# Where ScalarE's decode operations stand in an attention slot: attention and two feed-forward layers on one core

## The chip, the cores and the metric

The kernel runs on 1 core of one Trainium2 chip. The metric is the device time of one execution in microseconds; the value for a kernel is the median of its runs. Times of single instructions come from one profiled execution.

## What is computed

Block-causal attention (4 batches, 8 heads, 576 positions, head size 64) is followed by two feed-forward layers over 2304 tokens of width 512, each with a hidden width of 2048. All of it is float32.

```python
scores = scale * np.matmul(q, k.transpose(0, 1, 3, 2))
mask = block_i >= block_j                       # blocks of 64
scores = np.where(mask, scores, -1000000000.0)
attn = np.exp(scores - np.max(scores, axis=-1, keepdims=True))
attn = attn / (np.sum(attn, axis=-1, keepdims=True) + 1e-09)
x = np.matmul(attn, v)                          # then heads side by side: (2304, 512)
h = x @ w_in                                    # layer 1
x = (np.maximum(h, 0.0) + alpha * np.minimum(h, 0.0)) @ w_out
h = x @ w_in2                                   # layer 2
out = np.where(h > 0.0, h, np.exp(np.minimum(h, 0.0)) - 1.0) @ w_out2
```

## The kernel before

**Weights and their decode.** The host hands each weight matrix over as pairs of 32-bit words, two words to an element, the low one and the high one of a 64-bit number. The kernel makes of them two tiles in the matmul's own number format, a high part and a low part. It does so in 64 pieces of 128 x 512 elements (16 hidden chunks, two layers, `w_in` and `w_out`), each by one call of `load_w`. A piece is a load (SyncE's queue, tile `wraw`, three buffers) and then eight operations on three engines, in this order: ScalarE's `Abs` of the high words into the word tile `wword` (line 133) and its conversion of the low words in place (line 134), together `first`; VectorE's two bit operations (`bits`, lines 138 and 139) and the sign (`sign`, line 143); GpSimd's addition (`rounded`, line 148); ScalarE's cast to the high part `w` (line 158); VectorE's subtraction for the low part (`last`, through line 89). The `wraw` buffer is free again after GpSimd's addition, the `wword` buffer after the subtraction. There are two `wword` buffers.

**When the operations are written.** `later(ticks, emit)` puts an operation off by so many ticks. A tick ends with each attention slot, and with each step of the feed-forward work. So in the attention part `first` of a piece stands at the end of one slot, `bits` and `sign` at the end of the next, `rounded` at the end of the one after, the cast at the end of the fourth and the subtraction at the end of the fifth.

**Attention.** 64 slots, each one tile of scores of one pair of heads. `slot(k)` writes, in this order: the scores on TensorE (into one of two PSUM tiles, `twin`); the products of probabilities and values of an earlier slot (`second`, line 423); the transposes of an earlier slot's probabilities (`transposes`); the parts of late keys; `normalise` of an earlier slot (VectorE's sum and reciprocal, GpSimd's scaling of `p`); the maxima on VectorE (line 298); the held gates of layer 1; the output of the products, which is ScalarE's cast to `x` (line 429) and VectorE's low part (line 89); the copy `move` of the transposed probabilities `pt`, half on ScalarE and half on VectorE (lines 93 and 95); the exponentials on ScalarE (line 325); and what is planned for the slot's end, the due decode operations last. In this part the order of every engine is that in which the code is written. The first 16 slots are the short ones (two 128-row tiles of a pair); in the 48 that follow, tiles of 384, 512 and 576 columns take turns. From slot 14 on, `l1_beside` puts matmuls of layer 1 between the slots. Sixteen pieces of weights are decoded in the attention part, at the slots in `w_slots`.

**Feed-forward.** From about 258 us on only TensorE's order is the one written; on the other engines a scheduler, working with a model of the times when the kernel is built, puts the operations in order under the limits of the buffers. Layer 1 runs in passes A, B and D over units of 512 (one of 256) tokens, layer 2 in pass C. Each step multiplies one chunk (lines 551, 605), applies the gate (lines 528 to 535) or the exponential (609 to 614), and three steps later multiplies by `w_out` into one of five PSUM accumulators (lines 655, 630). At the end of a unit of pass A the four accumulators are copied out to `z` and `zl` (`to_z`, lines 93 on ScalarE and 95 on VectorE); at the end of a unit of B or D they are added to the earlier sum (line 662 on VectorE). The next unit's second accumulator is one that such a copy has to empty first.

`later` and the point in `load_w` that the change concerns:

```python
lead = arrival[0]
later(lead, first)
...
later(lead + 3, lambda: act.copy(hi, word[0]))
later(lead + 4, last)
```

Of the kernel before, what the change touches and what calls it, by code (L numbers as in the profile page):

```python
# [9 lines left out]
F32 = mybir.dt.float32  # L10
# [4 lines left out]
ALU = mybir.AluOpType  # L15
# [4 lines left out]
P = 128  # L20
B, H, S, D = 4, 8, 576, 64
NT, DM, DFF = 2304, 512, 2048
# [14 lines left out]
def f32(ap):  # L37
    return ap.bitcast(F32)
# [3 lines left out]
def attention_moe_kernel(ctx: ExitStack, tc: tile.TileContext, qT, kT, v_a, v_b, w1, w2, alpha, out):  # L42
    nc = tc.nc
    pe, act, dve, pool_e = nc.tensor, nc.scalar, nc.vector, nc.gpsimd
# [4 lines left out]
    wraw_p = ctx.enter_context(pool("wraw", 2))  # L49
# [18 lines left out]
    def ring(name, *banks):  # L68
        rings[name] = list(banks)
# [18 lines left out]
    def low_part(eng, out, x, high):  # L88
        return {"v": dve, "p": pool_e}[eng].tensor_tensor(out=out, in0=x, in1=f32(high), op=ALU.subtract)  # L89

    def copy(eng, out, x, scale=None):
        if eng == "a":
            return act.copy(out, x) if scale is None else act.mul(out, x, scale)  # L93
        if eng == "v":
            return dve.tensor_copy(out, x) if scale is None else dve.tensor_scalar(out, x, scale, None, ALU.mult)
        return pool_e.tensor_scalar(out, x, 1.0 if scale is None else scale, 1.0, ALU.mult, ALU.mult)  # L96
# [6 lines left out]
    def later(ticks, emit):  # L103
        due.setdefault(tick[0] + ticks, []).append(emit)
# [13 lines left out]
    def load_w(layer, f, r):  # L118
        if r == 0:
            wt[layer, f] = w_pools[min(f // 4, 2)].tile([P, 2, 2 * DM], F32R, tag="w", name="w")  # L120
        t = wt[layer, f]
        raw = wraw_p.tile([P, 2 * DM], U32, tag="wraw", name="wraw", bufs=3)
        nc.sync.dma_start(out=raw, in_=(w1, w2)[layer][f, :, r * DM:(r + 1) * DM].bitcast(U32))
        pairs = raw.rearrange("p (n t) -> p n t", t=2)
        low, high = pairs[:, :, 0], pairs[:, :, 1]
        units = low.bitcast(I32)
        hi, lo = (t[:, k, r * DM:(r + 1) * DM] for k in range(2))
        word = []

        def first():  # L130
            w = wraw_p.tile([P, DM], F32, tag="wword", name="wword")
            word.append(w)
            act.activation(out=w, in_=high.bitcast(F32), func=AF.Abs)  # L133
            act.activation(out=units, in_=low, func=AF.Copy, scale=2.0 ** -29)

        def bits():
            w, wi = word[0], word[0].bitcast(U32)
            dve.tensor_scalar(w, w, F64_MIN, F64_MAX, ALU.max, ALU.min)  # L138
            dve.tensor_scalar(wi, wi, 3, 0x3FFFFFF8, ALU.logical_shift_left, ALU.bitwise_and)  # L139

        def sign():
            wi = word[0].bitcast(U32)
            dve.scalar_tensor_tensor(  # L143
                out=wi, in0=high, scalar=0xC0000000, in1=wi, op0=ALU.bitwise_and, op1=ALU.bitwise_or)

        def rounded():
            w = word[0].bitcast(I32)
            pool_e.tensor_tensor(out=w, in0=w, in1=units, op=ALU.add)  # L148

        def last():  # L150
            low_part("v", lo, word[0], hi)
            ready.add((layer, f, r))
        lead = arrival[0]
        later(lead, first)
        later(lead + 1, bits)
        later(lead + 1, sign)
        later(lead + 2, rounded)
        later(lead + 3, lambda: act.copy(hi, word[0]))  # L158
        later(lead + 4, last)

    arrival = [2]

    def w_in(layer, f, part, kc):
        assert (layer, f, 0) in ready
        return wt[layer, f][:, part, kc * P:(kc + 1) * P]
# [17 lines left out]
    ap2 = att.enter_context(pool("att2", 2))  # L183
# [18 lines left out]
        return d // 2, slice(4 * (d % 2), 4 * (d % 2) + 4)  # L202

    def raw_tiles():
        return [ap2.tile([P, S], F32, tag=f"{x}raw", name=f"{x}raw", bufs=4) for x in "qk"]

    def load_early(d):
        b, hs = duo(d)
# [15 lines left out]
    def load_late(n):  # L224
        b, p = PAIRS[n]
        st[n]["raw"] = q, k = raw_tiles()
        hs = slice(2 * p, 2 * p + 2)
        nc.sync.dma_start(out=k, in_=kT[b, hs].rearrange("e p s -> (e p) s"))
        nc.sync.dma_start(out=q[:, 256:], in_=qT[b, hs].rearrange("e p s -> (e p) s")[:, 256:])

    def load_late_v(n):
        b, p = PAIRS[n]
# [5 lines left out]
    def high_parts(n):  # L238
        s = st[n]
        q, k = s["raw"]  # L240
        for which, x, scale in (("q", q[:, 256:], 0.125), ("k", k, None)):
            s[which] = [ap2.tile([P, x.shape[1]], F32R, tag=f"{which}{t}", name=f"{which}{t}") for t in "hl"]
            copy("p", s[which][0], x, scale)
        low_part("p", s["k"][1], k, s["k"][0])

    def low_parts(n):
        s = st[n]
        hi, lo = s["q"]
        dve.scalar_tensor_tensor(out=lo, in0=s["raw"][0][:, 256:], scalar=0.125, in1=f32(hi), op0=ALU.mult, op1=ALU.subtract)

    def diagonal(n):
        for low in range(2):
# [41 lines left out]
    def maxima(n, i):  # L294
        s = st[n]
        s["stat", i] = stat = stats[AT[n, i] % len(stats)]
        sb = s["sb", i]
        peak = lambda out, x, axis=AX.X: dve.tensor_reduce(out=out, in_=x, axis=axis, op=ALU.max, negate=True)  # L298
        if i == EARLY:
            dve.memset(sb[:64].rearrange("p x (t c) -> p x t c", t=2)[:, :, :, 64:P], NEG)  # L300
            for t, lo, hi in EARLY_TILES:
                peak(stat[:, 2 * t:2 * t + 2], sb[:, :, lo:hi])
        elif i < 4:
            ext = P * (i + 1)
            dve.memset(sb[:64, :, ext - 64:ext], NEG)
            peak(stat[:, 0:2], sb[:, :, :ext])
        else:
            peak(stat[:, 0:1], sb[:, :, :S // 2], AX.XY)
# [133 lines left out]
    for n in range(NP):  # L442
        k = AT[n, EARLY]
# [3 lines left out]
        for i in (2, 3, 4):  # L447
            k = AT[n, i]
# [12 lines left out]
    for n in range(NP):  # L461
        k = NP + 3 * n
# [10 lines left out]
    held = []  # L473

    def slot(k):
        here = SEQ[k] if k < NS else None
        if here:
            scores(*here)
        shared.clear()
        outs = [p() for p in products_at.get(k, ())]  # L480
        move = transposes(*transposes_at[k]) if k in transposes_at else None
        for emit in SPLITS.get(k, ()):
            emit()
        for emit in NORM.get(k, ()):
            emit()
        if here:
            maxima(*here)
        after = [h() for h in held]
        held.clear()
        for o in outs:  # L490
            o()
        if move:
            move()
        if here:
            exponentials(*here)
        for a in after:
            a()
        for emit in other_at.get(k, ()):
            emit()
        end_tick()  # L500
# [168 lines left out]
    with tc.manual_schedule(engines={ET.PE, ET.Activation, ET.DVE, ET.Pool, ET.SP}):  # L669
        ring("s", 0, 1)  # L670
        ring("t", 4, 5, 6, 7)

        halves = [(0, f, r) for r in range(2) for f in range(FA)]
        load_early(0)
        load_early(1)
        for half in range(2):
            scale_early(0, slice(256 * half, 256 * half + 256), "v")
        load_early_v(0)
        load_alpha()
        for emit in other_at[-1]:  # L680
            emit()
        load_early_v(1)
        end_tick()
        LEAD = 14
        stretches = [(LEAD, 22, 22, 30), (30, 39, 39, X_DONE[2]), (X_DONE[2], 59, 59, LAST)]
        w_slots = {1, 3, 6, 8, 10, 12, 14, 16}
        w_slots |= {27 + 5 * i for i in range(8)}
        halves += [(0, FA + f, r) for r in range(2) for f in range(4)]

        def slots(lo, hi):  # L690
            for k in range(lo, hi):
                if k in w_slots:
                    arrival[0] = 4 if k > 21 else 2
                    load_w(*halves.pop(0))
                slot(k)

        slots(0, LEAD)

        k = LEAD
        for u, (a, b, c, d) in enumerate(stretches):  # L700
            assert a >= X_DONE[u]
            parts = l1_beside(u)
            for first, end, n in ((a, b, 2 * FA), (c, d, 2 * KC)):
                slots(k, first)
                k = first
                for j in range(n):
                    next(parts)
                    to = first + (2 * (j + 1) * (end - first) + n) // (2 * n)
                    slots(k, to)
                    k = to  # L710
        arrival[0] = 2
        assert not held and not halves


    with tc.manual_schedule(engines={ET.PE}):
# [20 lines left out]
        for i in range(16):  # L736
            f, r = divmod(i, 2)
# [3 lines left out]
        for i in range(len(steps) + lag):  # L741
# [3 lines left out]
            if i < len(steps):  # L745
                k, u, f = steps[i]
                if f == fs[k][1]:
                    n = units.index((k, u)) + 1
# [4 lines left out]
            if i >= lag:  # L753
                k, u, f = steps[i - lag]
# [37 lines left out]
```

## Time and profile before

| | |
|---|---|
| median of 3 runs | 1006.86 us (1006.80 to 1007.06) |
| the profiled execution's own time | 1007.81 us |
| its span | 1006.0 us |
| TensorE matmul busy | 961.3 us (96%), 5008 matmuls |
| VectorE busy | 541.1 us (54%) |
| ScalarE busy | 441.9 us (44%) |
| GpSimd busy | 343.9 us (34%) |
| granted TensorE clock, mean | 0.989 |

The span is the time between the first and the last instruction of the profile; the execution's own time has 1.8 us around it. Busy shares are means over parts with different limits, so the argument goes by stretches of the span: from the start to about 70 us, on to the end of attention at about 258 us, and the feed-forward part behind it. In a list of instructions the columns are the start, the time, the engine, the line and operation with the tiles written and read, and in brackets the idle time of the engine just before with the engine and line that ended it.

### The profile page before, as it was taken

How to read it: one execution, taken by the hardware profiler on the slowest of the kernel's cores; microseconds unless marked ns; L12 is line 12 of the kernel's file. 1: busy time of each engine (PE TensorE's matmuls, PEld its weight loads, DVE VectorE, ACT ScalarE, POOL GpSimd, SP SyncE). 2: the span in 40 equal slices, each digit the busy share in tenths (PEclk: the TensorE clock that was granted, in tenths of full speed). 3: DMA queues.
4: the chain of work that ended last, by engine and by line, in shares of the span. 5: the costliest groups of instructions: out<-in, count | busy, mean ns of one | idle time of the engine just before them, and what ended most of it. 6: DMA issues, size and time to landing. Idle time of an engine off the chain costs nothing.

```text
span 1006.0 us, 13778 instructions
## 1 busy us (share of the span) xinstructions
PE 961.3 (96%) x5008; PEld 774.1 (77%) x5008; DVE 541.1 (54%) x1012; ACT 441.9 (44%) x985; POOL 343.9 (34%) x401
## 2 busy tenths in 40 slices
PE   5789999999997999999999999999999999999997
PEld 3456777666787788888889887888888888888896
DVE  5878676776498871311862489634333333333343
ACT  6876576776465653222553365422222222222222
POOL 4788576694255553322553363200000000000000
PEclk9999999999998999999999999999999999999999
DMA  6553533625546552401535555002002100200010
GB/s 216 178 183 140 154 102 114 224 72 157 183 140 237 199 183 84 141 0 42 186 119 177 163 201 174 29 1 111 15 1 84 42 1 1 84 1 0 1 43 21
DMA packets 55525, 105.76 MB, mean 105 GB/s; under 512 B 11041, under 2 KB 29473, under 8 KB 54305
## 3 DMA queue, kind: packets, MB, share of 16 engines
q1 hardware_dynamic: 55168, 104.62, 31.4%
q8 instruction: 39, 0.64, 0.3%
q10 hardware_dynamic: 288, 0.26, 0.1%
q14 instruction: 30, 0.24, 0.1%
HBM read 76.55 MB, written 28.31 MB: 104 GB/s over the span
## 4 chain that ended last, share of the span: by engine, by line
PE 73%; DVE 11%; ACT 6%; DMA 4%; POOL 3%; issue 2%; SPq 0%; POOLq 0%; ACTq 0%; DVEq 0%
PE bank L630 20%; PE bank L605 19%; PE bank L655 11%; PE bank L551 11%; PE bank L423 3%; PE bank L582 3%; DMA wraw<-w 2%; DVE w L89 2%; PE bank L570 2%; DVE wword L143 2%; PE pair L276 2%; DVE wword L139 2%; PE bank L363 2%; DVE wword L138 1%; ACT wword L133 1%
## 5 line engine op out<-in xcount | busy, mean ns | idle before, releaser
L605 PE MATMUL bank<-x,w 128*128 128x512 f32 (+1 forms) x960 | 210.4, 368 | 0.0
L605 PEld LDWEIGHTS bank<-x,w 128*128 128x128 f32 x960 | 169.7, 189 | 31.4
L551 PE MATMUL bank<-x,w 128*128 128x512 f32 (+1 forms) x816 | 177.2, 367 | 1.3 <-DVE xtail L89 1.3
L551 PEld LDWEIGHTS bank<-x,w 128*128 128x128 f32 x816 | 143.0, 191 | 26.2 <-ACT xtail L429 1.4
L610 DVE TENSOR_SCALAR e<-e 128x512 f32<-128x512 f32 (+1 forms) x80 | 33.1, 413 | 172.1 <-ACT e L609 172.1
L609 ACT ACTIVATE e<-bank 128x512 f32<-128x512 f32 (+1 forms) x80 | 44.4, 555 | 184.8 <-PE bank L605 184.8
L148 POOL TENSOR_TENSOR wword<-wword,wraw 128x512 int32<-128x512 int32 x64 | 93.7, 1465 | 77.3 <-issue 23.5
L531 DVE SCALAR_TENSOR_TENSOR g<-neg,beta,bank 128x512 f32<-128x512 f32 (+1 forms) x80 | 55.1, 689 | 117.8 <-ACT neg L528 117.7
L630 PE MATMUL bank<-w,gsl 128*128 128x512 f32 x432 | 106.4, 393 | 2.2 <-DVE z L662 2.2
L630 PE MATMUL bank<-w,gs 128*128 128x512 f32 x432 | 104.6, 389 | 0.0
L655 PE MATMUL bank<-gsl,w 128*128 128x512 f32 (+1 forms) x408 | 91.0, 371 | 9.1 <-ACT z L93 6.5
L96 POOL TENSOR_SCALAR p<-p,stat 128x128 f32<-128x128 f32 (+4 forms) x144 | 81.3, 580 | 48.5 <-DVE stat L334 32.7
L630 PEld LDWEIGHTS bank<-w,gsl 128*128 128x128 f32 x432 | 81.2, 190 | 19.5 <-DVE z L662 2.6
L630 PEld LDWEIGHTS bank<-w,gs 128*128 128x128 f32 x432 | 80.6, 188 | 16.4
L89 POOL TENSOR_TENSOR gs<-g,gs 128x512 fp32r<-128x512 f32 (+1 forms) x46 | 59.0, 1283 | 90.0 <-ACT gs L535 89.9
L655 PEld LDWEIGHTS bank<-gsl,w 128*128 128x128 f32 x408 | 71.7, 192 | 23.0 <-ACT z L93 7.1
L325 ACT ACTIVATE p<-pair,stat 128x128 f32<-128x128 f32 (+4 forms) x144 | 78.3, 557 | 24.0 <-DVE stat L298 21.7
L655 PE MATMUL bank<-gs,w 128*128 128x512 f32 (+1 forms) x408 | 87.8, 364 | 0.0
L655 PEld LDWEIGHTS bank<-gs,w 128*128 128x128 f32 x408 | 70.6, 189 | 12.2
L528 ACT ACTIVATE neg<-bank 128x512 f32<-128x512 f32 (+1 forms) x80 | 44.1, 552 | 79.5 <-PE bank L551 78.3
L89 DVE TENSOR_TENSOR w<-wword,w 128x512 fp32r<-128x512 f32 x64 | 57.1, 896 | 16.5 <-ACT w L158 15.9
L298 DVE TENSOR_REDUCE stat<-pair 128x2 f32<-128x256 f32 (+3 forms) x80 | 63.1, 806 | 4.2 <-PE pair L281 2.2
(80 smaller groups left out, 1256.7 us busy)
## 6 DMA issues: line engine op xcount, KB each, us to landing
wraw<-w SPq DMA_DIRECT2D x64, 512.0 KB, 4.0
xd<-x SPq DMA_DIRECT2D x4, 2048.0 KB, 8.5
x<-xd SPq DMA_DIRECT2D x16, 512.0 KB, 7.6
x<-yd SPq DMA_DIRECT2D x4, 2048.0 KB, 7.9
vraw<-v_a SPq DMA_DIRECT2D x24, 256.0 KB, 3.3
kraw<-kT SPq DMA_DIRECT2D x16, 288.0 KB, 3.8
yd<-gs SPq DMA_DIRECT2D x8, 512.0 KB, 3.7
yd<-gsl SPq DMA_DIRECT2D x8, 512.0 KB, 5.4
```

Source lines behind the costliest of these rows:

```text
L89: return {"v": dve, "p": pool_e}[eng].tensor_tensor(out=out, in0=x, in1=f32(high), op=ALU.subtract)
L96: return pool_e.tensor_scalar(out, x, 1.0 if scale is None else scale, 1.0, ALU.mult, ALU.mult)
L148: pool_e.tensor_tensor(out=w, in0=w, in1=units, op=ALU.add)
L298: peak = lambda out, x, axis=AX.X: dve.tensor_reduce(out=out, in_=x, axis=axis, op=ALU.max, negate=True)
L325: act.activation(out=out, in_=x, func=AF.Exp, bias=stat[:, k:k + 1], accum_out=stat[:, SUMS + 2 * k:SUMS + 2 * k + 1])
L528: act.activation(out=neg, in_=h, func=AF.Relu, scale=-1.0)
L531: dve.scalar_tensor_tensor(out=g, in0=neg, scalar=beta[:, f:f + 1], in1=h, op0=ALU.mult, op1=ALU.add)
L551: pe.matmul(h, w_in(0, f, wp_, kc), x[:, xp_, kc, :n], start=kc == 0 and t == 0, stop=kc == KC - 1 and t == 2)
L605: pe.matmul(h, w_in(1, f, wp_, kc), x[:, xp_, kc, :], start=kc == 0 and t == 0, stop=kc == KC - 1 and t == 2)
L609: act.activation(out=e, in_=h, func=AF.Exp)
L630: pe.matmul(acc, gs[:, gp_, tg * P:(tg + 1) * P], w_out(1, f, wp_, 0, DM), start=f == 0 and t == 0, stop=f == NF - 1 and t == 2)
L655: pe.matmul(acc, w_out(0, f, wp_, m * P, P), gs[:, gp_, :n], start=first and t == 0, stop=last and t == 2)
```

## The change

`first` and the cast of a piece no longer stand at a slot's end. When they come due, they are put on a list `amid`; the next slot writes what is on the list between `move` and the exponentials. The bit operations, the sign and the addition come due as many ticks after `first` as before, the subtraction one tick after the cast. Outside the attention slots (`in_slots` false) the list is passed by and the operations are written at once. Beside that the word tile has three buffers in place of two, and the raw query tile is 512 columns wide in place of 576, which makes the room: late queries go to columns 0 to 319 in place of 256 to 575.

```diff
         def first():
-            w = wraw_p.tile([P, DM], F32, tag="wword", name="wword")
+            w = wraw_p.tile([P, DM], F32, tag="wword", name="wword", bufs=3)
...
-        lead = arrival[0]
-        later(lead, first)
-        later(lead + 1, bits)
-        later(lead + 1, sign)
-        later(lead + 2, rounded)
-        later(lead + 3, lambda: act.copy(hi, word[0]))
-        later(lead + 4, last)
+
+        def begin():
+            first()
+            later(1, bits)
+            later(1, sign)
+            later(2, rounded)
+            later(3, lambda: between(cast))
+
+        def cast():
+            act.copy(hi, word[0])
+            later(1, last)
+        later(arrival[0], lambda: between(begin))
 
     arrival = [2]
+    amid, in_slots = [], [True]
+
+    def between(emit):
+        if in_slots[0]:
+            amid.append(emit)
+        else:
+            emit()
...
-        return [ap2.tile([P, S], F32, tag=f"{x}raw", name=f"{x}raw", bufs=4) for x in "qk"]
+        return [ap2.tile([P, n], F32, tag=f"{x}raw", name=f"{x}raw", bufs=4) for x, n in (("q", 512), ("k", S))]
...
-        nc.sync.dma_start(out=q[:, 256:], in_=qT[b, hs].rearrange("e p s -> (e p) s")[:, 256:])
+        nc.sync.dma_start(out=q[:, :320], in_=qT[b, hs].rearrange("e p s -> (e p) s")[:, 256:])
...
         if move:
             move()
+        todo = amid[:]
+        amid.clear()
+        for emit in todo:
+            emit()
         if here:
             exponentials(*here)
...
-        assert not held and not halves
+        assert not held and not halves and not amid
+        in_slots[0] = False
```

Three places show what it does to ScalarE's order. TensorE's order is the same in both kernels.

The first is slot 8, where the cast of one piece and `first` of another fall together. `x` is the cast of the products' output, `pt` the copy of transposed probabilities, `p` the exponentials. ScalarE before:

```order
L325 ACTIVATE p_406,stat_124<-pair_102,stat_124 128x256 x2
L158 CAST w<-wword 128x512
L133 ACTIVATE wword<-wraw 128x512
L134 ACTIVATE wraw<-wraw 128x512
L429 CAST x_318<-bank_105 128x256
L93 COPY pt<-bank_106 128x2x256
L325 ACTIVATE p_446,stat_125<-pair_101,stat_125 128x128 x2
```

The same place of ScalarE now (the lines have other numbers: 158 is 162, 325 is 337, 429 is 441):

```order
L337 ACTIVATE p_406,stat_124<-pair_102,stat_124 128x256 x2
L441 CAST x_315<-bank_105 128x256
L93 COPY pt<-bank_106 128x2x256
L162 CAST w<-wword 128x512
L133 ACTIVATE wword<-wraw 128x512
L134 ACTIVATE wraw<-wraw 128x512
L337 ACTIVATE p_446,stat_125<-pair_101,stat_125 128x128 x2
```

The three decode operations moved behind `x` and `pt`; the same operations stand ahead of the exponentials as before.

The second is slot 17, on ScalarE as well (`neg` and `gs` belong to layer 1). Before:

```order
L528 ACTIVATE neg<-bank_103 128x512
L158 CAST w<-wword 128x512
L133 ACTIVATE wword<-wraw 128x512
L134 ACTIVATE wraw<-wraw 128x512
L429 CAST x_655<-bank_105 128x256
L93 COPY pt<-bank_104 128x2x256
L325 ACTIVATE p_879,stat_128<-pair_102,stat_128 128x512 x2
```

And now:

```order
L544 ACTIVATE neg<-bank_103 128x512
L441 CAST x_654<-bank_105 128x256
L93 COPY pt<-bank_104 128x2x256
L162 CAST w<-wword 128x512
L133 ACTIVATE wword<-wraw 128x512
L134 ACTIVATE wraw<-wraw 128x512
L337 ACTIVATE p_879,stat_128<-pair_102,stat_128 128x512 x2
```

Here too the cast of the decode (158, now 162) no longer stands ahead of `x` and `pt`.

The third is in pass A, where the scheduler sets the order: ScalarE around the copies `z` of the 512-token unit's accumulators. Before:

```order
L133 ACTIVATE wword<-wraw 128x512
L134 ACTIVATE wraw<-wraw 128x512 x2
L528 ACTIVATE neg<-bank_2977 128x256
L93 COPY z<-bank_2971 128x512
L158 CAST w<-wword 128x512
L535 CAST gsl<-g 128x256
L93 COPY z<-bank_2973 128x512
```

And now:

```order
L133 ACTIVATE wword<-wraw 128x512
L134 ACTIVATE wraw<-wraw 128x512
L544 ACTIVATE neg<-bank_2977 128x256
L162 CAST w<-wword 128x512
L93 COPY z<-bank_2971 128x512
L93 COPY z<-bank_2973 128x512
L551 CAST gsl<-g 128x256
```

A cast of the decode moved ahead of the first `z`, and the second `z` ahead of the gate's cast. Counted from the start of pass A to VectorE's first copy `zl` of this unit, VectorE's order holds 26 bit operations, 12 signs and 13 subtractions now, 22, 11 and 11 before. From there to the first `zl` of the 256-token unit it holds 16, 9 and 9 now, 16, 7 and 8 before; and from the two subtractions that open pass D's second unit to the first addition of line 662 at its end, 23, 11 and 13 now, 21, 10 and 11 before.

## Rows read from the trace of the kernel before

**Rows 1.** Stretches; columns: TensorE, weight loads, VectorE, ScalarE, GpSimd busy, clock, DMA.

```profile
100.00:150.00 50.00, 49.85 (x338) 35.87 (x335) 35.27 (x88) 33.15 (x89) 34.38 (x49) 1.00 0.44 127
```

**Rows 2.** VectorE in order of time, low parts of the attention output (line 89).

```profile
22.74 0.42 DVE L89 TENSOR_TENSOR x<-bank,x 128x256 fp32r<-128x256 f32 x1 [1.09 <-ACT x L429]
...
33.57 0.42 DVE L89 TENSOR_TENSOR x<-bank,x 128x256 fp32r<-128x256 f32 x1 [1.38 <-ACT x L429]
...
41.27 0.42 DVE L89 TENSOR_TENSOR x<-bank,x 128x256 fp32r<-128x256 f32 x1 [0.85 <-ACT x L429]
...
74.61 0.42 DVE L89 TENSOR_TENSOR x<-bank,x 128x256 fp32r<-128x256 f32 x1 [4.58 <-ACT x L429]
```

**Rows 3.** ScalarE in order of time, slot 8 and one later exponential.

```profile
31.52 0.63 ACT L158 CAST w<-wword 128x512 fp32r<-128x512 f32 x1
...
32.02 0.69 ACT L133 ACTIVATE wword<-wraw 128x512 f32<-128x512 f32 x1
...
32.59 0.69 ACT L134 ACTIVATE wraw<-wraw 128x512 int32<-128x512 uint32 x1
...
33.17 0.37 ACT L429 CAST x<-bank 128x256 fp32r<-128x256 f32 x1
...
33.42 0.61 ACT L93 COPY pt<-bank 128x512 f32<-128x512 f32 x1
...
38.14 0.37 ACT L325 ACTIVATE p<-pair,stat 128x128 f32<-128x128 f32 x1 [1.74 <-DVE stat L298]
```

**Rows 4.** ScalarE in order of time, the cast of slot 17.

```profile
72.57 0.62 ACT L158 CAST w<-wword 128x512 fp32r<-128x512 f32 x1 [4.47 <-POOL wword L148]
```

**Rows 5.** GpSimd in order of time, the addition that this cast needs.

```profile
71.25 1.29 POOL L148 TENSOR_TENSOR wword<-wword,wraw 128x512 int32<-128x512 int32 x1
```

**Rows 6.** TensorE in order of time, its waits from 70 to 100 us.

```profile
70.08 1.70 PE L356 MATMUL bank<-ident,p 128*128 128x128 f32 x6 [1.90 <-POOL p L96]
...
80.50 1.66 PE L570 MATMUL bank<-x,w 128*128 128x512 f32 x6 [0.46 <-DVE stat L332]
...
87.58 1.67 PE L582 MATMUL bank<-gs,w 128*128 128x512 f32 x6 [0.67 <-DVE x L89]
```

**Rows 7.** Waits of TensorE, 259 to 620 us: total us, times, longest.

```profile
PE bank L655 <- ACT z L93: 6.5, 2, 4.9
PE bank L630 <- DVE z L662: 2.2, 1, 2.2
PE bank L655 <- DVE zl L95: 1.7, 2, 0.9
PE bank L551 <- DVE xtail L89: 1.3, 1, 1.3
```

**Rows 8.** Stretches ahead of three late accumulator copies, columns as in rows 1.

```profile
277.00:316.00 39.00, 34.08 (x174) 29.09 (x173) 33.85 (x44) 23.40 (x42) 22.35 (x17) 0.98 0.52 175
316.00:350.00 34.00, 31.61 (x195) 28.39 (x194) 28.54 (x42) 21.34 (x43) 20.07 (x16) 0.93 0.65 219
574.00:616.00 42.00, 40.66 (x180) 33.34 (x178) 37.56 (x52) 25.38 (x45) 22.03 (x16) 1.00 0.54 191
```

**Rows 9.** VectorE by line, 277 to 316 us: busy us, mean ns; idle before.

```profile
L139 DVE TENSOR_SCALAR wword<-wword 128x512 uint32<-128x512 uint32 x10 | 9.3, 928 | 0.3
L143 DVE SCALAR_TENSOR_TENSOR wword<-wraw,wword 128x512 uint32<-128x512 uint32 x10 | 9.0, 896 | 0.2
L89 DVE TENSOR_TENSOR w<-wword,w 128x512 fp32r<-128x512 f32 x9 | 8.6, 951 | 1.9 <-ACT w L158 1.7
L138 DVE TENSOR_SCALAR wword<-wword 128x512 f32<-128x512 f32 x9 | 6.0, 668 | 2.8 <-ACT wword L133 2.6
```

**Rows 10.** VectorE in order of time, one bit operation alone and one later.

```profile
298.97 0.43 DVE L139 TENSOR_SCALAR wword<-wword 128x512 uint32<-128x512 uint32 x1
...
302.37 1.41 DVE L139 TENSOR_SCALAR wword<-wword 128x512 uint32<-128x512 uint32 x1
```

**Rows 11.** GpSimd in order of time at the later one.

```profile
302.01 1.48 POOL L89 TENSOR_TENSOR gs<-g,gs 128x512 fp32r<-128x512 f32 x1
```

More of the change, by code (lines that the diff above doesn't have):

```diff
@@ L240, in high_parts @@
         q, k = s["raw"]
-        for which, x, scale in (("q", q[:, 256:], 0.125), ("k", k, None)):
+        for which, x, scale in (("q", q[:, :320], 0.125), ("k", k, None)):
             s[which] = [ap2.tile([P, x.shape[1]], F32R, tag=f"{which}{t}", name=f"{which}{t}") for t in "hl"]
@@ L248, in low_parts @@
         hi, lo = s["q"]
-        dve.scalar_tensor_tensor(out=lo, in0=s["raw"][0][:, 256:], scalar=0.125, in1=f32(hi), op0=ALU.mult, op1=ALU.subtract)
+        dve.scalar_tensor_tensor(out=lo, in0=s["raw"][0][:, :320], scalar=0.125, in1=f32(hi), op0=ALU.mult, op1=ALU.subtract)
     def diagonal(n):
```

## Prediction

> **What bounds the kernel now.** I read the busy time by stretches first, since the share over the whole span hides the answer: TensorE is busy 96% of 1006.0 us, so all that any change can give back without removing matmuls lies in the places where TensorE still waits. From about 70 us on it runs almost without a gap: 49.85 of 50 us in a stretch in the middle of attention [rows 1]. Before that, in slots 4 to 16 (about 18 to 70 us), the slots are short and the loop of VectorE and ScalarE sets the pace. There I read VectorE in order of time and look for the low part of the attention output, which needs ScalarE's `x`. In three slots it had to wait for it, 1.09, 1.38 and 0.85 us, and once later, in slot 17, 4.58 us [rows 2]. ScalarE's own list shows why: in slot 8 a cast, `Abs` and a conversion stand ahead of `x` [rows 3]; in slot 17 the cast itself waits 4.47 us for GpSimd [rows 4], whose addition began at 71.25 and took 1.29 us [rows 5]. Last I read TensorE's waits behind attention. They are few: 6.5 us for ScalarE's `z`, 1.7 for VectorE's `zl`, 2.2 for an addition of line 662, 1.3 for `xtail` [rows 7].
>
> **Slots 4 to 16.** The move takes one or three operations away from in front of `x` and puts them behind `pt`. The work stays the same, and so does what stands ahead of the exponentials, so these aren't later by it. What can be won is VectorE's wait for `x`: 1.09 + 1.38 + 0.85 = 3.32 us in three slots [rows 2]. What can be lost is on the other side: the bits of a piece, written a tick after its `first`, may meet an `Abs` that is not done. I followed slot 8. ScalarE is free for it at 31.52; from start to start, `x` takes 0.25, the cast 0.50, `Abs` 0.57 [rows 3], and `pt` has 0.61, so `Abs` ends near 31.52 + 0.25 + 0.61 + 0.50 + 0.69 = 33.6 at the latest. VectorE ends its maxima at about 33.57 - 1.38 = 32.2, then has its low part of `x` (0.42), its half of `pt` and the subtraction of an earlier piece, together some 1.3 us, an estimate from the 0.42 of rows 2 and about 0.4 each for the two others, as the quickest operation on a tile of this size [rows 10]. It is at the next bits near 33.5. So nothing of weight stands against the 1.38. ScalarE's delay is slack too: a later exponential waits 1.74 us for VectorE's maxima [rows 3]. In slots where `first` alone moves I take 0.1 us off for bits that come early, three times. **Take 3.0 us**; bounds 0 (another wait of the loop, for the maxima, takes over at once) and 3.3.
>
> **Slot 17.** With `x` and `pt` ahead of the cast, VectorE's 4.58 us [rows 2] are free of ScalarE's wait, but what counts from here is TensorE. It had waited 1.90 us for GpSimd's `p` at 70.08, which the move doesn't touch, and its next waits are 0.46 at 80.50 and 0.67 at 87.58, both for VectorE [rows 6]. VectorE gets 4.58 us earlier at most, more than either wait, so I take both: 0.46 + 0.67 = **1.1 us**. Bounds 0 and 4.6, the latter if GpSimd and VectorE, no longer behind, also bring the matmuls before 70.08 forward. New behind the cast is the exponential of slot 17: it waits if GpSimd's addition (end 71.25 + 1.29 = 72.54) is late. The same cast stood ahead of it before, so it loses nothing.
>
> Together 3.0 + 1.1 = 4.1 us, bounds 0 and 7.9. As TensorE is full from there [rows 1], a start that is earlier by so much should be carried to the end of attention and on.
>
> **The narrower query tile.** No cost: the late load moves the same 320 columns, and the operations read as many elements as before. A word tile takes 512 x 4 = 2,048 bytes in a partition, the four query tiles give back 4 x 64 x 4 = 1,024. In attention the weight loads keep their place in SyncE's queue.
>
> **The third word tile in the feed-forward part.** This is the part that may cost. A piece's `first` needs a free word tile; with three the scheduler puts decode work earlier, and front of three late copies of accumulators there is more of it. I count it by order and price it by the means of rows 9. Ahead of the 512-unit's `zl`: 4 bit operations more, 2 x (0.928 + 0.668) = 3.2; 1 sign 0.9; 2 subtractions 1.9; sum 6.0 us on VectorE, which had 39 - 33.85 = 5.15 idle there [rows 8]. Up to the 256-unit's `zl`: 2 signs and 1 subtraction, 1.8 + 0.95 = 2.75, against 5.46 idle. Ahead of line 662: 1.6 + 0.9 + 1.9 = 4.4 against 4.44 idle. In all 13.1 us more work, 15.05 us of idle time. The idle time is largely of the kind that the third tile removes: VectorE waits 2.6 us for ScalarE's `Abs` and 1.7 for the cast [rows 9]. So it should cover most. I take nine tenths: 13.1 x 0.1 = **1.3 us lost** in the waits of rows 7. Bounds: all uncovered, 13.1 lost; or a gain, if the deeper buffer brings decode ahead so far that the copies no longer stand behind it: at most the waits themselves, 6.5 + 1.7 + 2.2 = 10.4 us [rows 7].
>
> The means of rows 9 hold contention: the same bit operation took 0.43 us at 298.97 and 1.41 us at 302.37 [rows 10], the latter beside a GpSimd operation of 1.48 us [rows 11]. The Trainium skill, page "SBUF — State Buffer", section "SBUF: two separate sides", says that VectorE and GpSimd share a pair of ports as an exclusive lock, held for a whole instruction, the other being blocked. The rows just named agree. By it the added operations cost VectorE less wherever GpSimd happens to be idle (4 bits at 0.43 would be 1.7 in place of 3.2), and more where a denser VectorE meets it more often; the sum itself goes by the means.
>
> **Sum.** -3.0 - 1.1 + 1.3 = -2.8 us. The profiled execution of before took 1007.81 us (span 1006.0 and 1.8 around it), so its like is 1005.0; it lies 0.95 above the median of the runs, 1006.86, and on that scale the forecast is 1006.86 - 2.8 = **1004.1 us**.
>
> **Rivals.** *The third tile also ends the late-copy waits.* The copies `z`, `zl` and the additions stand in queues full of decode, and if that is done earlier they come on time. For it speaks that VectorE's idle time there is a wait for `Abs`, which a third tile removes; against it that more decode now stands ahead of the same copies. Half of 10.4 removed gives 1006.86 - 4.1 - 5.2 = 997.6, all of it 992.4. The Trainium skill, page "Perfetto Trace Analysis", section "Optimization Strategy", has the rule for it: a gap that repeats can mean too few buffers for the next tile. The trace bears it out in part, as said.
>
> *Slower: the extra decode ahead of the copies isn't covered.* Its place is VectorE and ScalarE ahead of the first `z` and `zl`, its price 13.1 us less what fits in the idle time. With half of it covered the loss is 6.55, and the time 1006.86 - 4.1 + 6.55 = 1009.3. It decides when less than 9.0 of the 13.1 us (0.69) is covered. For it: in the first stretch 6.0 us stand against 5.15 of idle time [rows 8], and an added ScalarE cast stands ahead of `z`. Against: part of that idle time is the wait that the third tile removes.
>
> *The attention gain comes to nothing.* The slots may be bound by something else that closes the gap at once (the maxima behind TensorE's scores), and TensorE behind slot 17 has 1.1 us of waits to give, no more. Or the end of attention is earlier and pass A's first stop, which waits 4.9 us for `z` [rows 7], eats it, since the decode chain sets that copy and not TensorE. Then only the 1.3 are left: 1008.2, within the measurement if the cover is whole (1006.9).
>
> **Chances.** Forecast 0.48, late-copy waits gone 0.17, uncovered decode 0.18, nothing from attention 0.17. Taken alone the forecast reaches from 1006.86 - 6.2 = 1000.7 (3.3 in the slots, 2.9 as the middle of 1.1 and 4.6 behind slot 17, decode covered whole) to 1006.86 - 3.0 + 3.9 = 1007.8 (nothing behind slot 17, seven tenths covered). Over all cases the range is 997.0 to 1009.5: it takes in the half of the second case and most of the third, and leaves out some 0.15. This kernel can be told from no change at about 0.2%, 2 us: faster means below 1004.85, which the forecast holds with 0.36 and the second case with 0.17, so 0.53; within 0.29; slower 0.18.
>
> **What would show it.** In the profile of the changed kernel: VectorE's low part of `x` without a wait in slots 5, 8 and 10, and in slot 17; TensorE's matmul of 70.08 about 3 us earlier and the waits of 80.50 and 87.58 gone; attention ending near 254 in place of 258 us; VectorE's busy time in the stretches of rows 8 some 3 to 6 us higher and its wait for `Abs` mostly gone; the waits of rows 7 about as long in sum, 10 to 13 us. I'm wrong on the slots if bits now wait for `Abs` as long as VectorE waited for `x`; on the carrying if attention ends earlier and the `z` wait grows by as much; and on the third tile if the waits of rows 7 sum to under 7 or over 16 us.

## The result and the profile after

The changed kernel takes 1014.81 us (median of 6 runs, 1011.15 to 1017.65), the kernel before 1006.44 in the runs beside it: a ratio of 1.0088 with an interval of 1.0065 to 1.0111. It is slower by 0.9%, where 1004.1 us was forecast, and lies above the upper end of the range, 1009.5.

TensorE's order is the same in both kernels, so the start of one and the same matmul can be compared in two traces. The difference (after minus before, in us) shows where the time went:

| the same matmul, at ... us of before | 94.6 | 257.1 | 259.6 | 310.0 | 364.0 | 602.0 | 633.6 and to the end |
|---|---|---|---|---|---|---|---|
| after | -5.2 | -7.1 | -2.5 | -1.0 | +2.1 | +2.1 | +7.3 |

Attention gained 7.1 us. The feed-forward part lost 14.4: 4.6 at its very first matmul, 1.5 on the way to 310 us, 3.1 around the copies of the accumulators, 5.2 at the additions of pass D. Each loss is at one of TensorE's stops (a stop is a wait of TensorE), or in the slower matmuls behind one: the granted clock is 0.57 from 253 to 261 us and 0.63 from 616 to 630, the rows of which stand with the one-tile kernel below. Its waits in the profile of the changed kernel, from 252 to 630 us (in total, times, longest), answer to [rows 7]:

```profile
PE bank L671 <- ACT z L93: 9.3, 2, 5.5
PE bank L646 <- DVE z L678: 6.6, 1, 6.6
PE bank L567 <- DVE xtail L89: 5.8, 1, 5.8
PE bank L671 <- DVE zl L95: 1.4, 2, 1.2
PE bank L567 <- DVE g L547: 0.8, 1, 0.8
```

The wait for `xtail` grew from 1.3 to 5.8 us, that for the addition (line 662, now 678) from 2.2 to 6.6, those for `z` and `zl` from 8.2 together to 10.7. All listed in [rows 7] were 11.7, the same ones are now 23.1. The view of [rows 7] has one wait more, 0.9 us for `gsl`, which is now 0.5.

VectorE in order of time, the low parts of `x` in slots 5, 8, 10 and 17, against [rows 2]:

```profile
20.86 0.42 DVE L89 TENSOR_TENSOR x<-bank,x 128x256 fp32r<-128x256 f32 x1
...
30.81 0.41 DVE L89 TENSOR_TENSOR x<-bank,x 128x256 fp32r<-128x256 f32 x1
...
37.91 0.41 DVE L89 TENSOR_TENSOR x<-bank,x 128x256 fp32r<-128x256 f32 x1
...
68.12 0.42 DVE L89 TENSOR_TENSOR x<-bank,x 128x256 fp32r<-128x256 f32 x1 [1.16 <-ACT x L441]
```

The waits of 1.09, 1.38 and 0.85 us are gone, and 4.58 has become 1.16. What the slots were to give, they gave. TensorE's own row there (the matmul that stood at 70.08 in [rows 6]) is earlier, though its wait for GpSimd's `p` is longer:

```profile
67.00 1.70 PE L368 MATMUL bank<-ident,p 128*128 128x128 f32 x6 [2.50 <-POOL p L96]
```

Last, stretches of the changed kernel, columns as in [rows 1]; the last line is that of [rows 8]'s last, between the same matmuls:

```profile
100.00:150.00 50.00, 49.17 (x323) 35.84 (x323) 36.84 (x91) 34.59 (x93) 33.45 (x48) 1.00 0.39 115
277.00:316.00 39.00, 32.23 (x165) 27.02 (x163) 37.12 (x48) 24.10 (x45) 23.97 (x18) 0.99 0.60 195
576.10:622.50 46.40, 40.69 (x180) 33.38 (x178) 44.78 (x57) 27.49 (x49) 22.50 (x17) 0.96 0.55 185
```

VectorE had 4.44 us idle ahead of the last copy before; now 1.62 in a stretch that is 4.4 us longer. Its busy time there went from 37.56 to 44.78, so by 7.2 us, where the order had led me to 4.4.

### The profile page after: what moved, and what is told of

It reads as the page before. It is cut to its first block, busy times and chain, and to the rows that moved or that the text cites. A ratio compares the mean times of both kernels' runs of the same rounds, so it can differ in the third digit from the quotient of the medians.

```text
span 1013.3 us, 13823 instructions
## 1 busy us (share of the span) xinstructions
PE 964.3 (95%) x5008; PEld 777.1 (77%) x5008; DVE 552.3 (55%) x1012; ACT 440.8 (44%) x985; POOL 341.7 (34%) x401
## 4 chain that ended last, share of the span: by engine, by line
PE 75%; DVE 11%; ACT 4%; DMA 4%; POOL 3%; issue 3%; SPq 0%; POOLq 0%; DVEq 0%; ACTq 0%
PE bank L646 20%; PE bank L621 18%; PE bank L671 11%; PE bank L567 11%; PE bank L435 4%; PE bank L598 3%; PE bank L586 3%; DVE w L89 2%; DVE wword L143 2%; DMA wraw<-w 2%; PE pair L288 2%; PE bank L375 2%; DVE wword L139 2%; DVE wword L138 1%; PE pair L293 1%
## 5 line engine op out<-in xcount | busy, mean ns | idle before, releaser
L148 POOL TENSOR_TENSOR wword<-wword,wraw 128x512 int32<-128x512 int32 x64 | 91.2, 1427 | 84.5 <-DVE wword L143 19.8
L89 DVE TENSOR_TENSOR w<-wword,w 128x512 fp32r<-128x512 f32 x64 | 67.9, 1075 | 8.6 <-ACT w L162 7.7
```

## Experiments

Two theories stood against each other: the third word tile costs in the feed-forward part, by the decode that it lets the scheduler put ahead of copies; or the earlier end of attention costs, because loads and decode don't come earlier with it. The table gives each kernel's difference to before at the same matmuls, from one profile each, and the measured times.

| kernel | 94.6 | 257.1 | 259.6 | 310.0 | 364.0 | 602.0 | to the end | median us | ratio to before, interval |
|---|---|---|---|---|---|---|---|---|---|
| e1 tile alone | -0.3 | +0.9 | +1.4 | +3.9 | +6.7 | +6.7 | +10.5 | 1019.53 | 1.0146 (1.0131 to 1.0162) |
| e2 two tiles behind attention | -2.3 | -4.1 | -4.1 | -3.9 | -6.3 | -6.3 | -6.6 | 999.51 | 0.9948 (0.9933 to 0.9963) |
| e4 `first` alone moved | -1.5 | -1.9 | -1.9 | -1.6 | -3.7 | -3.7 | -4.9 | 1003.24 | 0.9982 (0.9971 to 0.9992) |
| e5 cast alone moved | -3.3 | -4.4 | -4.4 | -3.3 | -5.7 | -5.7 | -5.6 | 1001.67 | 0.9971 (0.9957 to 0.9986) |
| e6 three for layer 2 | -3.1 | -5.0 | -5.0 | -2.3 | -6.3 | -6.3 | -1.2 | 1004.59 | 0.9982 (0.9969 to 0.9996) |
| e8 three from the ninth piece | -5.3 | -7.3 | -7.3 | -6.4 | -5.3 | -5.3 | -0.4 | 1008.07 | 1.0018 (1.0006 to 1.0030) |
| e9 one tile behind attention | -4.9 | -6.7 | -6.7 | -7.4 | -20.2 | -17.7 | -22.0 | 987.22 | 0.9810 (0.9779 to 0.9841) |
| e10 short additions | -5.3 | -7.2 | -6.8 | -5.3 | -5.8 | -5.8 | -8.6 | 1002.41 | 0.9965 (0.9942 to 0.9988) |
| e12 before, one tile | +0.2 | +2.4 | +2.4 | +1.3 | -2.9 | -2.9 | -7.3 | 999.66 | 0.9922 (0.9893 to 0.9951) |

**The third tile without the move.** From the kernel before:

```diff
-            w = wraw_p.tile([P, DM], F32, tag="wword", name="wword")
+            w = wraw_p.tile([P, DM], F32, tag="wword", name="wword", bufs=3)
```

and the narrower query tile as in the change.

> The kernel before with the third word tile and the narrower query tile, but every decode operation written at a slot's end as before. Theory (the third tile in the feed-forward part is what costs): attention ends within 0.5 us of before, TensorE's stops behind it sum to about 24 us as in the changed kernel, against 12.5 before; time 1006.4 + 10 to 14.5, so 1016 to 1021 us. Rival (the earlier end of attention costs, since loads and decode don't come earlier with it; the tile is harmless): 1005 to 1008 us.

1019.53 us: slower than the changed kernel itself, as the first theory has it. Attention ends 0.9 us later, so nothing is earlier, and the feed-forward part loses all the same. The rival falls. The wait for `xtail`, though, is only 1.8 us here, so the 5.8 need the earlier attention as well.

**The move without the third tile behind attention.** From the changed kernel; in attention the pieces still take turns on three tiles:

```diff
-            w = wraw_p.tile([P, DM], F32, tag="wword", name="wword", bufs=3)
+            third = in_slots[0] and words_taken[0] % 3 == 2
+            words_taken[0] += 1
+            w = wraw_p.tile([P, DM], F32, tag="word3" if third else "wword", name="wword", bufs=1 if third else 2)
...
-    amid, in_slots = [], [True]
+    amid, in_slots, words_taken = [], [True], [0]
```

> The changed kernel with three word tiles in the attention slots only; the feed-forward pieces take turns on two. Theory: attention gains 7.2 us as in the changed kernel, the first matmul of pass A waits again for work that doesn't get earlier, 1 to 5 us, the later stops are those of before; time 999 to 1003 us. Rival (the earlier end of attention costs): the stops of the changed kernel remain, 1012 to 1016 us.

999.51 us. Its waits of TensorE from 250 to 620 us are nearly those of [rows 7]; `z` has 5.6 us in place of 6.5, with the same longest one:

```profile
PE bank L673 <- ACT z L93: 5.6, 2, 4.9
PE bank L648 <- DVE z L680: 2.1, 1, 2.1
PE bank L673 <- DVE zl L95: 1.9, 2, 1.0
PE bank L569 <- DVE xtail L89: 1.3, 1, 1.3
```

So a start that is 4.1 us earlier is carried through: the stop of 4.9 us for `z` moves with it and doesn't eat it. Two things came out otherwise than expected: attention gained 4.1 us and not 7.2, and the wait for `xtail` didn't grow.

**Which half of the move.** Both from e2, with one of the two operations back at the slot's end:

```diff
-            later(3, lambda: between(cast))
+            later(3, cast)
```

> As e2, but only the first operations of a piece (Abs and conversion) are written between the copy and the exponentials; the cast is written at a slot's end as before. Theory (what is won in slots 4 to 16 is VectorE's wait for x, shared between both; behind slot 17 it is the cast alone): about 2 us won at 70 us, nothing more at 95 us; VectorE's wait of 4.6 us in slot 17 stays; time 1002 to 1006 us. Rival (the gain is that of the third tile and of first alone): time within 1 us of e2.

```diff
-        later(arrival[0], lambda: between(begin))
+        later(arrival[0], begin)
```

> As e2, but only the cast is written between the copy and the exponentials; Abs and conversion stand at a slot's end as before. Theory: about 1 to 2 us won at 70 us, 1 to 2 more by 95 us since the wait of slot 17 is gone; time 1001 to 1005 us. Rival (the gain is that of first alone): within 1 us of before, 1005.5 to 1007.5.

1003.24 and 1001.67 us: in these two profiles the cast is worth 4.4 us of attention, `first` 1.9. The sizes agree with what was expected, one reading doesn't: with `first` alone moved VectorE's wait in slot 17 fell too, to 1.15 us, where 4.6 had been expected to stay. Whether the two gains add up can't be read from single profiles: with both, these gave 4.1 (e2) to 7.3 us (e8), with the same attention order but for its last slots. By the medians, against 1004.91 us for the kernel before beside them, `first` alone gained 1.7 us, the cast alone 3.2 and both 5.4, so the two nearly add up. What differs between the profiles lies before 72 us, where e2 was 0.1 us ahead and the changed kernel 3.4. TensorE has stretches at half clock (1.2 GHz) there, at other places in each profile: e2 has two, where the changed kernel has none (granted clock 0.79 from 18 to 26 us and from 52 to 60 us, against 1.00). Over the matmuls of before from 20.2 to 22.9 us and from 53.8 to 58.5 us e2 falls back by 1.5 us each, the changed kernel by 0.3 and 0.0. That is 2.7 of the 3.3 us; why the clock fell there in the one and not in the other was not tested.

**Whose stop is whose.** Three tiles for layer 2's pieces only, and three from the ninth feed-forward piece on, so that the end of attention is ordered as with two. As e2, with

```diff
+            third = words_taken[0] % 3 == 2 and (in_slots[0] or layer == 1)
```

> The changed kernel with three word tiles in attention and for layer 2's pieces, and two for the layer 1 pieces of the feed-forward part. Theory (each stop belongs to the decode ahead of its own copy): the stops up to 360 us are those of the two-tile kernel e2 (1.3 for xtail, 4.9 and 1.0, 0.7 and 0.9), the stop at line 678's addition is that of the changed kernel, 6.6 in place of 2.1; e2's time of 999.5 + 4.5 to 5, so 1003 to 1005.5 us. Rival (the stops hang together, the late one follows from the earlier ones): the late stop stays near 2.1 and the time within 1.5 us of 999.5.

and with

```diff
+            third = words_taken[0] % 3 == 2 and (in_slots[0] or words_taken[0] >= 24)
```

> The changed kernel with three word tiles in attention and from the ninth feed-forward piece on; the first eight take turns on two, so that ScalarE has two conversions of later pieces ahead of the last x, as before, and not three. Theory (the 5.8 us wait for xtail is the third of these conversions, which waits for its load): that wait goes back to about 1.3 us, the stops behind it stay as in the changed kernel; 1014.8 - 3.5 to 5, so 1009.5 to 1011.5 us. Rival (attention's end is held by the loads whatever the order): the wait stays at 4 us or more, 1013 to 1016 us.

TensorE's waits in e6, from 252 to 620 us:

```profile
PE bank L648 <- DVE z L680: 6.5, 1, 6.5
PE bank L673 <- ACT z L93: 4.2, 2, 3.4
...
PE bank L569 <- DVE xtail L89: 1.3, 1, 1.3
```

and in e8, from 250 us on:

```profile
PE bank L673 <- ACT z L93: 7.6, 2, 5.3
PE bank L648 <- DVE z L680: 6.6, 1, 6.6
PE bank L569 <- DVE xtail L89: 1.3, 1, 1.3
```

The stop at the addition is layer 2's third tile alone (e6 1004.59, expected 1003 to 1005.5). The stop at `xtail` is that of the first pieces: with them on two tiles it is 1.3 us again. e8 gained more than the 3.5 to 5 us expected (1008.07), since its later stops also came out shorter. What the stop at `xtail` consists of stands in ScalarE's list of the changed kernel, at the end of attention:

```profile
251.28 0.66 ACT L134 ACTIVATE wraw<-wraw 128x512 int32<-128x512 uint32 x1 [2.17 <-DMA wraw<-w]
255.31 0.65 ACT L134 ACTIVATE wraw<-wraw 128x512 int32<-128x512 uint32 x1 [3.37 <-DMA wraw<-w]
255.87 0.35 ACT L441 CAST x<-bank 128x256 fp32r<-128x256 f32 x1
256.12 0.21 ACT L441 CAST xtail<-bank 128x64 fp32r<-128x64 f32 x1
```

and in its chain of the work that ended last:

```profile
249.08 6.15 DMA wraw<-w
```

A conversion of a later piece, which the third tile let in ahead of the last `x`, waits for a load that was issued at 249.08 and took 6.15 us. `x` itself had its sums by 251.3 and stood behind it. The order alone doesn't make the stop: in e10 below the same three conversions stand ahead of the last `x`, but the load starts at 246.67 and takes 4.34 us, the conversion waits 0.74, and the stop is 1.7. In both kernels the load starts behind the second of two of GpSimd's additions, which free `wraw` buffers: they take 3.42 us from 245.64 in the changed kernel and 0.99 from 245.52 in e10, where they are short.

**One tile.** If decode ahead of the copies sets the stops, less of it must shorten them. From the changed kernel, attention again on three:

```diff
+            pair = in_slots[0] and words_taken[0] % 3 > 0
+            words_taken[0] += 1
+            w = wraw_p.tile([P, DM], F32, tag="word2" if pair else "wword", name="wword", bufs=2 if pair else 1)
```

> The changed kernel with three word tiles in attention and only one for the feed-forward pieces: VectorE's order then has 46 bit operations in place of 58 (two tiles) or 64 (three) ahead of the copy of the 512-token unit, and 110 in place of 121 or 125 ahead of line 678's addition. Theory (decode ahead of the copies sets the stops): the stops at z, zl and line 678 fall from 4.9 + 1.0, 0.7 + 0.9 and 2.1 to under 1 us each, and if no weights come late the time is 999.5 - 7 to 12, so 987 to 993 us; weights that come late would show as waits of TensorE for w, with their own price. Rival (the stops have another cause, or decode with one tile is too slow for layer 1): the z stop stays at 3 us or more, or waits for w take its place, 998 us or more.

987.22 us, the best of all, 1.9% below before. TensorE's waits from 250 us to the end:

```profile
PE bank L673 <- DVE zl L680: 1.9, 1, 1.9
PE bank L569 <- DVE xtail L89: 1.3, 1, 1.3
PE bank L673 <- POOL gsl L89: 0.2, 1, 0.2
```

The stops for `z`, `zl` and the addition of pass D's second unit are gone, no weight came late, and one new stop of 1.9 us stands elsewhere. In all its waits are 3.4 us, where the kernel before had 12.6 (`gsl` counted), so 9.2 less; the feed-forward part gained 15.3. The 6.1 us that are left I put down to the clock: after its longer stops TensorE ran at half clock (1.2 GHz) for a while, as the 0.93 of [rows 8] already showed, and without them it didn't. Stretches at such stops, granted clock third from the end; the kernel before, at the copies of the 512-token unit and at the additions of pass D:

```profile
313.00:321.00 8.00, 4.56 (x20) 4.27 (x21) 7.87 (x13) 6.24 (x13) 4.15 (x4) 0.57 0.60 188
...
614.00:625.00 11.00, 8.80 (x31) 6.52 (x31) 11.00 (x15) 6.90 (x13) 5.28 (x4) 0.84 0.36 131
```

the changed kernel, at the first matmul of pass A and at the additions of pass D:

```profile
253.00:261.00 8.00, 3.93 (x11) 3.19 (x12) 0.56 (x2) 1.70 (x4) 0.00 (x0) 0.57 0.86 337
...
616.00:630.00 14.00, 7.40 (x22) 5.45 (x21) 14.00 (x21) 8.78 (x16) 5.83 (x5) 0.63 0.22 75
```

and e9 at the same three places:

```profile
252.00:260.00 8.00, 7.09 (x31) 5.93 (x32) 2.02 (x4) 1.92 (x5) 0.23 (x1) 1.00 0.86 324
300.00:308.00 8.00, 8.00 (x63) 7.73 (x63) 5.00 (x9) 5.11 (x11) 3.48 (x4) 1.00 0.58 200
594.00:605.00 11.00, 11.00 (x51) 9.09 (x49) 10.77 (x17) 6.63 (x12) 4.64 (x3) 1.00 0.67 251
```

**Count or length.** VectorE's busy time ahead of pass D's additions had grown by more than the operations that were added. VectorE by line in that stretch (busy us, mean ns, idle before); before, 574 to 616 us:

```profile
L143 DVE SCALAR_TENSOR_TENSOR wword<-wraw,wword 128x512 uint32<-128x512 uint32 x10 | 8.9, 890 | 0.2
L138 DVE TENSOR_SCALAR wword<-wword 128x512 f32<-128x512 f32 x11 | 8.6, 783 | 3.7 <-ACT wword L133 3.4
L89 DVE TENSOR_TENSOR w<-wword,w 128x512 fp32r<-128x512 f32 x11 | 7.8, 715 | 2.2 <-ACT w L158 2.2
L139 DVE TENSOR_SCALAR wword<-wword 128x512 uint32<-128x512 uint32 x10 | 7.0, 700 | 0.3
```

and after, 576.1 to 622.5 us:

```profile
L89 DVE TENSOR_TENSOR w<-wword,w 128x512 fp32r<-128x512 f32 x13 | 13.3, 1051 | 2.2 <-ACT w L162 2.2
L143 DVE SCALAR_TENSOR_TENSOR wword<-wraw,wword 128x512 uint32<-128x512 uint32 x11 | 11.5, 1044 | 0.2
L139 DVE TENSOR_SCALAR wword<-wword 128x512 uint32<-128x512 uint32 x11 | 9.5, 862 | 0.3
L138 DVE TENSOR_SCALAR wword<-wword 128x512 f32<-128x512 f32 x12 | 7.0, 582 | 0.1
```

32.3 us in 42 operations became 41.3 in 47. At the means of before the 47 would take 13 x 0.715 + 11 x 0.890 + 11 x 0.700 + 12 x 0.783 = 36.2: so 3.9 us are count and 5.1 are length. The long ones stand beside a GpSimd operation: of all VectorE operations in the two stretches 9 took more than 1 us before and 16 after, each of them while GpSimd was at work. To tell whether this matters for the stop, GpSimd's additions were cut short in the feed-forward part of the changed kernel:

```diff
-            pool_e.tensor_tensor(out=w, in0=w, in1=units, op=ALU.add)
+            n = DM if in_slots[0] else 64
+            pool_e.tensor_tensor(out=w[:, :n], in0=w[:, :n], in1=units[:, :n], op=ALU.add)
```

> The changed kernel, but in the feed-forward part GpSimd's addition takes 64 of a piece's 512 columns (the rounding of the other 448 is left out). VectorE's order then has 128 bit operations, 63 signs and 62 subtractions ahead of line 678's addition, more than the 125, 62 and 61 of the changed kernel. Theory (what fills VectorE there is for the larger part the lengthening of its operations beside GpSimd's additions): VectorE's operations fall back to their lengths alone (0.43, 0.69 and 0.68 us), and the stop at that addition falls from 6.6 to under 2.5 us though more decode stands ahead; time 1014.8 - 6 to 14, so 1001 to 1009 us. Rival (the count of operations ahead sets the stop): it stays at 6.6 us or more, and the time at 1010 or above.

The same view of it, 568.2 to 608.7 us:

```profile
L89 DVE TENSOR_TENSOR w<-wword,w 128x512 fp32r<-128x512 f32 x14 | 11.1, 823 | 4.8 <-ACT w L163 4.8
L143 DVE SCALAR_TENSOR_TENSOR wword<-wraw,wword 128x512 uint32<-128x512 uint32 x12 | 8.4, 699 | 0.2
L138 DVE TENSOR_SCALAR wword<-wword 128x512 f32<-128x512 f32 x13 | 7.3, 560 | 0.6 <-ACT wword L133 0.2
L139 DVE TENSOR_SCALAR wword<-wword 128x512 uint32<-128x512 uint32 x12 | 5.1, 422 | 0.2
```

and its waits of TensorE from 250 us:

```profile
PE bank L672 <- ACT z L93: 8.6, 2, 4.7
...
PE bank L647 <- DVE z L679: 0.6, 1, 0.6
```

51 operations take 31.9 us, less than the 42 of before, and the stop falls from 6.6 to 0.6 us with more decode ahead of it. Four operations are still over 1 us, so the subtraction (823 ns) and the first bit operation (560) aren't down to the 0.68 and 0.43 that were expected. So at this place the length, which goes with the meetings with GpSimd, makes the stop, and not the count. A shorter addition also hands its piece on sooner, but that isn't what VectorE gained by: it waits longer for the cast here than in the kernel before (4.8 us against 2.2). The `z` stops remain (8.6 us), and the chain ahead of the longer one, 4.7 us at 344.6, leads back along ScalarE's queue to a load: an `Abs` at 339.83 had waited 4.99 us for it. For the other it is not settled by this run, since a shorter addition also lets the scheduler put the rest in another order.

**Do the two gains add up?** From the kernel before, with two tiles in attention and one behind it:

```diff
+            other = in_slots[0] and words_taken[0] % 2 == 1
+            words_taken[0] += 1
+            w = wraw_p.tile([P, DM], F32, tag="word2" if other else "wword", name="wword", bufs=1)
```

> The kernel before with one word tile for the feed-forward pieces (two in attention, decode operations at a slot's end as before). Theory (the attention gain and the feed-forward gain add up): attention as before, the feed-forward part as in e9, so e9's time of 987.2 plus the 5 to 7 us of attention, 992 to 994.5 us. Rival (the stops of the feed-forward part take back what attention gives, so that the move is worth nothing with one tile): within 1.5 us of 987.2.

999.66 us; neither number was right. The stops of pass D are gone as in e9, but one for `z` appeared at 346.8 us, 5.7 us long. ScalarE's list shows it to be of the kind of `xtail`, a conversion that waits for its load, with four more operations and then `z` behind it:

```profile
342.21 0.65 ACT L136 ACTIVATE wraw<-wraw 128x512 int32<-128x512 uint32 x1 [6.30 <-DMA wraw<-w]
...
346.33 0.36 ACT L93 COPY z<-bank 128x256 f32<-128x256 f32 x1
```

One tile helps without the move (ratio 0.9922), but what the move is worth with one tile can't be read from this pair.

## Why the prediction was wrong, step by step

*Slots 4 to 16 and slot 17* were right in mechanism and too small in size. The three waits went, and slot 17's by three quarters; forecast 4.1 us, measured 4.1 to 7.3 in the profiles with this order, bounds 0 to 7.9. At 94.6 us the changed kernel is 5.2 us ahead. I had not looked at the later slots, where the same cast stood ahead of `x` and `xtail`: another 1.9 us by 257 us. TensorE's waits at 80.50 and 87.58 [rows 6] are gone, as forecast. The price on the other side was read too low, though nothing came of it: the subtraction taken at 0.4 us took 0.68 in slot 8 of the kernel before and 0.88 in the changed one, but from 15 to 75 us the bits wait 1.4 us for `Abs` in all, where they had waited 2.0.

*The narrower tile* cost nothing that shows; with it, e1 stays within 0.4 us of before from 83 to 233 us.

*The carrying.* The rival in which pass A's first stop eats the gain "since the decode chain sets that copy and not TensorE" is refuted by e2: the 4.9 us came 4 us earlier. That rival had the right place in view and the wrong copy. What ate 4.6 of the 7.1 us was the stop at `xtail`, the first wait of the part, to which I gave no growth at all. One more conversion stands ahead of the last `x`. It takes 0.65 us itself; its price is the 3.37 us that it waits for its load, which started only when GpSimd had freed a buffer. I priced moved work only by busy time.

*The third tile* is the step that failed: "I take nine tenths: 13.1 x 0.1 = 1.3 us lost". The feed-forward part lost 14.4 us. Leaving out `xtail`, 9.8 remain, of which 7.3 are longer waits (2.5 for `z` and `zl`, 4.4 for the addition, 0.8 for `g`, less 0.4 for `gsl`) and about 2.5 half clock behind the stops in the main, an estimate, being what is left. VectorE's busy time grew by 18.0 us where the order had led me to 13.1: 41.8 to 47.5 from pass A's first matmul to the end of its stop for `z`, 27.9 to 33.0 from there to the end of the next, and the 7.2 of pass D. Two things were wrong in the term.

The cover: VectorE's idle time ahead of pass D's additions fell by 2.8 us (4.44 to 1.62), and 4.4 us stood out of 7.2. At the first two copies 1.0 of 5.7 us and 1.6 of 5.1 came out as longer stops, so over all three 7.0 of 18.0, and 0.61 was covered where I took 0.9 (the half clock and the wait for `g` left aside). The 1.6 are not VectorE's work alone: the `z` stop of the 256-token unit stands behind an `Abs` that had waited for its load, 1.82 us before (at 345.34) and 2.41 after (at 347.26).

The price: the work grew by 7.2 us and not 4.4, because a VectorE that waits less for `Abs` (3.4 us ahead of pass D's additions before, at most 0.1 after) meets GpSimd more often: 16 operations over 1 us in place of 9 (GpSimd itself was busy for 22.03 us there [rows 8] and is for 22.50). I had the pair that shows it, 0.43 us alone and 1.41 beside [rows 10, 11], and wrote that a denser VectorE would meet it more often, but left the sum at the means of a less dense stretch. The Trainium skill, page "SBUF — State Buffer", section "SBUF: two separate sides", calls the shared pair of ports an exclusive lock, held for a whole instruction; e10 agrees, 422 ns for the bit operation where GpSimd's additions are short against 862.

*The rivals.* The slower one named the mechanism, place and threshold (less than 0.69 covered) and was the true one; its 1009.3 rested on half of 13.1 us, and `xtail` was not in it either. The faster one, that a third tile also ends the late copies, had it the wrong way round: the stops at those copies are shortened by fewer tiles, not more. The rule cited for it (the Trainium skill, "Perfetto Trace Analysis", "Optimization Strategy") was not borne out here: with 3, 2 and 1 tiles behind attention the kernel takes 1014.81, 999.51 and 987.22 us.

*The range* reached up to 1009.5 because the loss of `xtail` and the dearer operations were in no case at all. The sign named for a wrong third tile, waits of rows 7 above 16 us, is what came: 23.1.

## What to carry to other kernels

A deeper buffer for work that isn't urgent also lets more of it stand ahead of work that is. Where a scheduler fills in-order queues, count what it puts ahead of each late copy, price it by the lengths of a dense stretch, and ask of every operation that moved ahead what it waits for, above all a load. Then try a shallower buffer as well: here one tile in place of two or three removed almost all of TensorE's stops.

## What the hardware showed beside that

VectorE's operations on SBUF took about 0.42 us (bit operation) or 0.69 us (sign) alone and up to 1.5 and 1.7 us beside a GpSimd operation; the gate, which reads one operand from PSUM, kept its length. The sign in order of time, in the changed kernel:

```profile
605.45 1.67 DVE L143 SCALAR_TENSOR_TENSOR wword<-wraw,wword 128x512 uint32<-128x512 uint32 x1
...
613.31 0.69 DVE L143 SCALAR_TENSOR_TENSOR wword<-wraw,wword 128x512 uint32<-128x512 uint32 x1
```

with GpSimd beside the first of them:

```profile
605.09 1.48 POOL L89 TENSOR_TENSOR gs<-g,gs 128x512 fp32r<-128x512 f32 x1
```

The gate by line, ahead of pass D's additions, before (three of the four beside a GpSimd operation):

```profile
L531 DVE SCALAR_TENSOR_TENSOR g<-neg,beta,bank 128x512 f32<-128x512 f32 x4 | 3.0, 740 | 0.0
```

and after (one of the four):

```profile
L547 DVE SCALAR_TENSOR_TENSOR g<-neg,beta,bank 128x512 f32<-128x512 f32 x4 | 3.0, 742 | 0.0
```
